# One buffer of 544 tokens per two heads, and the global queries' scores of a batch in one stage

## The chip, the cores and the metric

One NeuronCore of a Trainium2 chip. Five engines run queues of their own, in order: TensorE (PE in the profile, with its weight loads as PEld), VectorE (DVE), ScalarE (ACT), GpSimd (POOL) and SyncE (SP, which issues the DMAs). The metric is the time of one execution in microseconds (us), the median of three runs.

## The reference

Eight batches of eight heads, 512 local tokens (block `l`) and 32 global ones (block `g`), head size 64. A global query sees all 544 keys; a local query sees the 32 global keys and the local keys within 32 positions. The result, 544 tokens by 512 channels, goes through a gated layer with a convolution over tokens:

```python
s_g = scale * np.matmul(q_g, k_all.transpose(0, 1, 3, 2))
out_g = np.matmul(sm(s_g), v_all)
...
s_ll = np.where(mask, s_ll, -1000000000.0)
...
out_l = np.matmul(a_l, np.concatenate([v_g, v_l], axis=2))
...
h = np.maximum(x @ w_in, 0.0)
...
    conv_out += conv_w[k][None, None, :] * hp[:, k:k + S, :]
gate = 1.0 / (1.0 + np.exp(-conv_out))
return (h * gate @ w_out).astype(np.float32)
```

The weights arrive as 64-bit floats and are split on the chip into a high and a low part; the two products of the layer are sums of three products of such parts.

## The kernel before, in words

All work is cut into steps with short names. Per head `n`: local scores S (`SC`, for two heads at once: 32 matmuls of 128 columns, each on one of eight 64x32 parts of the array), mask and minimum M (`MA`, VectorE), exponential E (`EX`, ScalarE), transpose T (`TR`), its copy A. Per two heads: the sums NS, the value product P (`PV`, 32 matmuls of 64 columns on 128x32 parts), scaling N, transpose U, and then the layer's input: XH copies a rounded high part (ScalarE) and XL subtracts it for the low part (VectorE), both out of PSUM. Before, this is done twice, for the first 242 and the last 274 local columns (YH and YL are the second), into tiles `xh` and `xl` of 274 columns, `HW`; 13 of each exist.

The global queries go by groups of four heads: LG loads the queries, padded with zeros for the other head of a pair; G (`G`) makes their scores against four heads' keys with eight matmuls over all 128 rows, on four 128x32 parts, into two PSUM banks; GM scales them and takes the minimum (VectorE), GE the exponential, GN the reciprocal sums, GT six transposes, GC copies, GP 24 value matmuls, GO the scaling, GQ and GX put the result into the first 32 columns of the first half's input.

The layer runs by halves of 272 tokens, eight hidden units each: Z (`Z`, PZ in the tables) is twelve matmuls of 274 columns for unit `u`; RE the relu (ScalarE), C1, Ca and Cb the convolution (GpSimd, then VectorE twice), TH, and for two units GG the gate, GH and GL its two parts. The output is O, for each of four channel tiles in two halves Oa and Ob of twelve matmuls, then OE (copy) and ST (store). Units are numbered through: unit 0 to 15 are batch 0.

The weights come in eight chunks: WD (load), WA (ScalarE), WC (three VectorE instructions, L119 to L123), WH (ScalarE), WL (four VectorE instructions, L126 to L134). Units of a half need the `w_in` chunks two by two.

What sets the order: `plan` lists every step with what it waits for and which slots it takes (`SLOTS`), `arranged` plays them with costs and the tables POS, POS0 and WPOS, and `emit` writes them to the engines' queues in the order found. All psum tiles share eight banks. POS0, WPOS and `late` serve batch 0, POS the others.

Of the kernel before, what the change touches and what calls it, by code (L numbers as in the profile page):

```python
# [52 lines left out]
def attn_moe(ctx: ExitStack, tc: tile.TileContext, qk_d, vw_d, qg_d, w_in_d, w_out_d, cw_d, out_d):  # L53
# [28 lines left out]

    corner = const.tile([P, 2, 4, SG], F32, name="corner")
    nc.gpsimd.memset(corner, 0.0)
    for k, sign in enumerate((1, -1)):
        nc.gpsimd.affine_select(
            out=corner[:, k], in_=corner[:, k], pattern=[[sign * SG, 4], [sign, SG]], compare_op=ALU.is_ge, fill=NEG,
            base=0, channel_multiplier=-sign,  # L90
        )
# [57 lines left out]
    nc.sync.dma_start(out=cwr.rearrange("p n w -> p (n w)"), in_=cw_d)  # L149
    cw = drop(cwr)  # L150
    if wpe == 2:
        cw = const.tile([P, 3 * NFT], F32, name="cw")
# [1 line left out]
        w0, w1, t = cwr[:, :, 0], cwr[:, :, 1], cw.bitcast(U32)
        magnitude(w1, t)
        scaled_bits(w1, t, 0x7FFFF8)
        power(cwp, t)
        rest("v", f(cwp), w0, w1, cwp, 0)
        nc.vector.tensor_tensor(out=cw, in0=cw, in1=f(cwp), op=ALU.add)
# [761 lines left out]
```

## Time and profile before

| | |
|---|---|
| median of 3 runs | 595.16 us (594.88 to 595.27) |
| the profiled execution | 595.32 us, its span 593.5 us |
| busy: PE, PEld | 560.9 us (95%), 528.8 us (89%) |
| busy: DVE, ACT, POOL | 424.0 us (71%), 324.2 us (55%), 101.1 us (17%) |
| mean granted TensorE clock | 0.982 |

The span is the time from the first to the last instruction of the profiled execution; the execution's own time lies a little above it. Busy shares are averages over stages. A row of a timeline gives start, length, engine, line, operation, tiles, shapes and, in brackets, an idle time ahead of it and what ended it; rows of PE merge neighbours, a float32 matmul other than a transpose stands as two records (the eight of a G as x16), and a length ends where the last result is out, a little after the next stage starts. The difference of two starts is what a stage holds its engine.

### The profile page before, as it was taken

The numbers are of one execution on the slowest core, as the hardware profiler recorded it, in microseconds if no ns is written. First come the engines' busy times: TensorE is split into PE (matmuls) and PEld (weight loads), VectorE is DVE, ScalarE is ACT, GpSimd is POOL, SyncE is SP. The second block draws the span as 40 slices with busy tenths as digits, with TensorE's granted clock in tenths as the row PEclk, the third lists the DMA queues.
The fourth block names the chain that finished last, engine by engine and source line by source line (L and its number), as shares of the span: only waits on it lengthen the run. The fifth ranks groups of instructions, "written<-read, shape, count | busy, mean of one in ns | idle before, by whom it ended". The sixth has DMA issues, their size and how long they took to land.

```text
span 593.5 us, 20757 instructions
## 1 busy us (share of the span) xinstructions
PE 560.9 (95%) x8704; PEld 528.8 (89%) x8704; DVE 424.0 (71%) x1388; ACT 324.2 (55%) x994; POOL 101.1 (17%) x190
## 2 busy tenths in 40 slices
PE   5656997999999999999999999999999999999997
PEld 3345896999999999999999999999999999999997
DVE  4999999689477948577685858668584856565651
ACT  4954794676477666446565655555565543333320
POOL 6000242033012111121111012111101212221210
PEclk9977999899999999999999999999999999999999
DMA  6987334156234332123333222232412000000001
GB/s 254 390 286 313 95 118 170 39 204 223 91 135 153 107 134 98 56 110 108 135 108 145 100 78 94 100 144 97 146 63 75 20 22 20 29 20 29 30 29 47
DMA packets 22125, 68.46 MB, mean 115 GB/s; under 512 B 2576, under 2 KB 12816, under 8 KB 21008
## 3 DMA queue, kind: packets, MB, share of 16 engines
q1 hardware_dynamic: 22032, 67.14, 31.2%
q8 instruction: 68, 1.11, 0.8%
q14 instruction: 25, 0.20, 0.1%
HBM read 58.22 MB, written 8.91 MB: 113 GB/s over the span
## 4 chain that ended last, share of the span: by engine, by line
PE 84%; DVE 9%; ACT 2%; issue 1%; DMA 1%; POOL 0%; DVEq 0%
PE ps_o L523 32%; PE ps_h L460 31%; PE ps_v L325 5%; PE ps_s L264 4%; PE ps_t L304 4%; PE pv L341 2%; PE psg L278 2%; PE go L422 2%; PE gt L406 1%; DVE pr L285 1%; DVE t L484 1%; DMA vf<-vw 1%; DVE wt L123 1%; DVE raw L132 1%; ACT pr L295 1%
## 5 line engine op out<-in xcount | busy, mean ns | idle before, releaser
L460 PE MATMUL ps_h<-xh,w_in 128*128 128x274 f32 x1024 | 225.4, 298 | 2.8 <-DVE raw L132 1.3
L523 PE MATMUL ps_o<-g,w_out 128*128 128x272 f32 x1536 | 212.2, 290 | 0.0
L523 PEld LDWEIGHTS ps_o<-g,w_out 128*128 128x128 f32 x1536 | 200.0, 189 | 0.2
L460 PEld LDWEIGHTS ps_h<-xh,w_in 128*128 128x128 f32 x1024 | 171.9, 191 | 6.3 <-ACT g L212 1.4
L248 POOL TENSOR_SCALAR t<-hb,cw 128x272 f32<-128x272 f32 x128 | 79.9, 629 | 425.7 <-ACT hb L469 159.2
L460 PE MATMUL ps_h<-xl,w_in 128*128 128x274 f32 x512 | 149.5, 292 | 0.8 <-issue 0.8
L484 DVE SCALAR_TENSOR_TENSOR t<-hb,cw,t 128x272 f32<-128x272 f32 x256 | 125.7, 514 | 30.5 <-POOL t L248 29.1
L295 ACT ACTIVATE pr<-pr,negm 128x128 f32<-128x128 f32 x256 | 99.5, 391 | 47.7 <-DVE negm L285 47.7
L469 ACT ACTIVATE hb<-ps_h 128x273 f32<-128x273 f32 x128 | 50.8, 398 | 93.4 <-PE ps_h L460 91.9
L460 PEld LDWEIGHTS ps_h<-xl,w_in 128*128 128x128 f32 x512 | 98.1, 192 | 1.0 <-issue 1.0
L285 DVE CUSTOM_DVE_ANT_0 pr<-ps_s,mask 128x128 f32<-128x128 f32 x256 | 57.8, 285 | 25.6 <-PE ps_s L264 23.2
L212 DVE COPY o<-ps_o 128x272 f32<-128x272 f32 x64 | 28.0, 438 | 54.8 <-PE ps_o L523 54.6
L212 ACT CAST g<-t 128x544 fp32r<-128x544 f32 x64 | 40.9, 646 | 34.5 <-DVE t L498 22.6
L498 DVE SCALAR_TENSOR_TENSOR t<-t,hb 128x544 f32<-128x544 f32 x64 | 46.0, 719 | 14.3 <-ACT t L493 13.3
L493 ACT ACTIVATE t<-t 128x544 f32<-128x544 f32 x64 | 42.4, 663 | 15.0 <-DVE t L484 13.9
L212 ACT COPY a<-ps_t 128x512 f32<-128x512 f32 x64 | 37.0, 583 | 23.2 <-PE ps_t L304 23.0
L295 ACT ACTIVATION_READ_ACCUMULATOR pr<-pr,negm 128x1 f32 x256 | 48.3, 189 | 0.0
L264 PE MATMUL ps_s<-qk 64*32 64x128 f32 x2048 | 38.4, 283 | 8.4 <-DMA qk<-qk 5.8
L304 PE MATMUL ps_t<-ident,pr 128*128 128x128 f32 x256 | 43.0, 282 | 3.5 <-ACT pr L295 2.5
L215 DVE TENSOR_TENSOR g<-t,g 128x544 fp32r<-128x544 f32 x56 | 41.0, 737 | 6.8 <-ACT g L212 5.3
L264 PEld LDWEIGHTS ps_s<-qk 64*32 64x32 f32 x2048 | 29.9, 109 | 12.7 <-DMA qk<-qk 5.8
L304 PEld LDWEIGHTS ps_t<-ident,pr 128*128 128x128 f32 x256 | 31.1, 144 | 8.2 <-ACT pr L295 7.6
(70 smaller groups left out, 466.1 us busy)
## 6 DMA issues: line engine op xcount, KB each, us to landing
vf<-vw SPq DMA_DIRECT2D x32, 896.0 KB, 6.3
qk<-qk SPq DMA_DIRECT2D x32, 592.0 KB, 4.9
out<-o SPq DMA_DIRECT2D x64, 136.0 KB, 1.7
raw<-w_in SPq DMA_DIRECT2D x4, 1024.0 KB, 6.6
raw<-w_out SPq DMA_DIRECT2D x4, 1024.0 KB, 6.6
qgf<-qg SPq DMA_DIRECT2D x16, 64.0 KB, 2.0
cwr<-cw SPq DMA_DIRECT2D x1, 24.0 KB, 1.9
```

Source lines behind the costliest of these rows:

```text
L212: nc.scalar.copy(out=out, in_=in_) if choice(key) == "a" else eng(key).tensor_copy(out=out, in_=in_)
L248: nc.gpsimd.tensor_scalar(out=out, in0=in_, scalar1=by, scalar2=0.0, op0=ALU.mult, op1=ALU.add)
L264: nc.tensor.matmul(heads[n + j]["s"][b * SG : (b + 1) * SG, t, :], lhsT=qk[rows, i * SG : (i + 1) * SG], rhs=qk[rows, a : a + P], start=Tr ...
L285: nc.vector.tensor_tensor_reduce(out=pr[:, t, :], in0=st["s"][:, t, :], in1=mask[:, t].rearrange("p a c -> p (a c)"), op0=ALU.add, op1=ALU ...
L295: nc.scalar.activation(out=st["p"][:, t, :], in_=st["p"][:, t, :], func=AF.Exp, scale=-1.0, bias=st["m"][:, t : t + 1], accum_out=two["r"] ...
L304: nc.tensor.transpose(out=st["t"][:, t, :], in_=st["p"][:, t, :], identity=ident)
L460: nc.tensor.matmul(ps, lhsT=w[:, ft, ct, :], rhs=x, start=i == 0, stop=i == 3 * NCT - 1)
L469: nc.scalar.activation(out=o, in_=z, func=AF.Relu, scale=0.5)
L484: nc.vector.scalar_tensor_tensor(out=st["t"], in0=st["h"][:, k : k + HALF], scalar=cw[:, 3 * ft + k : 3 * ft + k + 1], in1=st["t"], op0=AL ...
L493: nc.scalar.activation(out=t, in_=t, func=AF.Tanh)
L498: nc.vector.scalar_tensor_tensor(out=t, in0=t, scalar=1.0, in1=h, op0=ALU.add, op1=ALU.mult)
L523: nc.tensor.matmul(ps, lhsT=w[:, mt, ft, :], rhs=g[:, ft, :], start=ft + i == 0, stop=ft == NFT - 1 and i == 2)
```

## The change

The input of the layer gets one pair of tiles per two heads, 544 columns wide (`x_of`); XH and XL handle 512 columns at once, YH and YL go away, and a unit reads a slice. Six such pairs exist in place of 13 half tiles. The half with the later tokens is now taken first (`TURN`). G serves a whole batch: the queries are no longer padded, each matmul contracts the 64 rows of one head, and sixteen matmuls on eight 64x32 parts fill four banks. The two groups that come out have heads mixed by pair and parity, so GP of a group needs the copies GC of both. GN scales the exponentials themselves, ahead of GT, in place of the weights that GO used. The mask is built half by VectorE, the convolution's taps (`taps`) are converted after the first weight chunk, and POS, POS0, WPOS, LATE and STAY have new values throughout, so that the written order differs from the first instruction on. `WAY` is all "v": a second way of splitting weights is in the code and not taken.

```diff
+        e = nc.vector if t < 2 else nc.gpsimd
...
+                e.tensor_copy(out=mask[rows, t, k], in_=corner[rows, int(local > i), b])
...
-                nc.gpsimd.tensor_copy(out=mask[rows, t, k], in_=corner[rows, int(local > i), b])
...
+    def taps():
...
-    def x_of(b, ct, half):
-        if (b, ct, half) not in xs:
-            xs[b, ct, half] = (xp.tile([P, HW], F32R, name="xh"), xp.tile([P, HW], F32R, name="xl"))
-        return xs[b, ct, half]
-
-    def outputs(n, half):
-
+    def x_of(b, ct):
+        if (b, ct) not in xs:
+            xs[b, ct] = (xp.tile([P, S], F32R, name="xh"), xp.tile([P, S], F32R, name="xl"))
+        return xs[b, ct]
+
+    def XH(n):
         b, h = divmod(n, H)
-        xh, xl = x_of(b, h // 2, half)
-        if half == 0:
-            return heads[n]["pv"][:, 0 : HW - SG], xh[:, SG:HW], xl[:, SG:HW]
-        return heads[n]["pv"][:, SL - HW : SL], xh, xl
-
-    def XH(n, half):
-        pv, xh, xl = outputs(n, half)
-        cp("XH", xh, pv)
-
-    def XL(n, half):
-        pv, xh, xl = outputs(n, half)
-        nc.vector.tensor_tensor(out=xl, in0=pv, in1=f(xh), op=ALU.subtract)
+        cp("XH", x_of(b, h // 2)[0][:, SG:S], heads[n]["pv"])
+
+    def XL(n):
+        b, h = divmod(n, H)
+        xh, xl = x_of(b, h // 2)
...
-        gr = groups[n // 4] = {}
-        gr["qgf"] = load.tile([P, 4, SG], F32, name="qgf", bufs=SLOTS["qg"])
-        nc.sync.dma_start(out=gr["qgf"], in_=qg_d[b, h // 4])
+        qg[n // H] = load.tile([P, 4, SG], F32, name="qgf", bufs=SLOTS["qg"])
+        nc.sync.dma_start(out=qg[n // H], in_=qg_d[n // H])
...
     def G(n):
 
-        gr = groups[n // 4]
-        gr["s0"] = bank([P, 480], "psg0")
-        gr["s1"] = bank([P, 64], "psg1")
-        for i, ps in enumerate((gr["s0"], gr["s1"])):
-            for j in range(4):
-                k = heads[n - 3 + j // 2 * 2]["qk"][:, SL:]
-                k = k[:, 608:672] if i else k[:, 0:640].rearrange("p (a c) -> p a c", c=P)[:, :, 0:96]
-                nc.tensor.matmul(ps[j * SG : (j + 1) * SG], lhsT=gr["qgf"][:, j, :], rhs=k, start=True, stop=True)
+
+        first = n - 7
+        g = [groups.setdefault(2 * (n // H) + j, {}) for j in range(2)]
+        for i, (name, w) in enumerate((("s0", 480), ("s1", 64))):
+            for j in range(2):
+                g[j][name] = bank([P, w], f"psg{i}")
+            for c in range(4):
+                k = heads[first + 2 * c]["qk"][:, SL:]
+                for j in range(2):
+                    rows = slice(j * D, (j + 1) * D)
+                    kj = k[rows, 608:672] if i else k[rows, 0:640].rearrange("p (a c) -> p a c", c=P)[:, :, 0:96]
+                    nc.tensor.matmul(
+                        g[j][name][c * SG : (c + 1) * SG], lhsT=qg[n // H][rows, c, :], rhs=kj, start=True, stop=True
+                    )
...
-        gr["w"] = small.tile([P, 2], F32, name="gw", bufs=SLOTS["pg"])
-        nc.vector.tensor_scalar(out=gr["w"], in0=whose, scalar1=sums, scalar2=None, op0=ALU.mult)
+        nc.vector.tensor_scalar(out=gr["pg"], in0=gr["pg"], scalar1=sums, scalar2=None, op0=ALU.mult)
...
         po = gr["po"] = bank([P, D], "go")
-        for c in range(6):
+        b, h = divmod(first, H)
+        for k in range(6):
             for j in range(4):
-                own = slice(j * SG, (j + 1) * SG)
-                v = heads[first + j // 2 * 2]["vf"][:, j % 2, VALUES.index(ONCE[c]), :]
-                nc.tensor.matmul(po[own], lhsT=gr["pgt"][:, c, own], rhs=v, start=c == 0, stop=c == 5)
+                c = h // 2 + j // 2
+                v = heads[first + j // 2 * 2]["vf"][:, j % 2, VALUES.index(ONCE[k]), :]
+                nc.tensor.matmul(
+                    po[j * SG : (j + 1) * SG], lhsT=groups[2 * b + j % 2]["pgt"][:, k, c * SG : (c + 1) * SG], rhs=v,
+                    start=k == 0, stop=k == 5,
+                )
 
     def GO(n):
 
         gr = groups[n // 4]
-        og = gr["og"] = att.tile([P, 2, D], F32, name="og", bufs=SLOTS["pg"])
-        po, w = gr["po"], gr["w"]
+        og = gr["og"] = att.tile([P, 2, D], F32, name="og", bufs=SLOTS["og"])
         nc.vector.tensor_tensor(
-            out=og, in0=po[:, None, :].to_broadcast([P, 2, D]), in1=w[:, :, None].to_broadcast([P, 2, D]), op=ALU.mult
+            out=og, in0=gr["po"][:, None, :].to_broadcast([P, 2, D]), in1=whose[:, :, None].to_broadcast([P, 2, D]),
+            op=ALU.mult,
...
+    def half_of(hh):
+        return (hh + TURN) % 2
...
-            xh, xl = x_of(b, ct, half)
+            xh, xl = (x[:, half * (S - HW) : half * (S - HW) + HW] for x in x_of(b, ct))
...
-    ps=8, x=13, hb=2, qk=3, vf=3, qg=2, p=4, r=3, a=4, n=2, pg=1, pgt=1, t=2, o=2, wt=1, g0=2, g1=2,
+    ps=8, x=6, hb=2, qk=5, vf=3, qg=2, p=4, r=3, a=4, n=2, pg=2, pgt=2, og=2, t=2, o=2, wt=1, g0=2, g1=2,
...
-    LQ=-3.56, LG=-53.13, LV=12.71, S=-3.9, M=7.61, E=46.84, NS=-11.03, T=-16.54, A=-39.33, P=-1.74, N=0.2, U=-7.02,
...
+    LQ=-13.92, LG=-68.69, LV=2.61, S=-2.17, M=37.43, E=93.64, NS=-82.9, T=-1.82, A=-40.59, P=-24.11, N=-52.26,
...
+TURN = 1
+
+WAY = "vvvvvvvv"
...
-            for half, x in enumerate("XY"):
-                name = f"x{b},{h // 2},{half}"
-                at_n(x + "H", [("U", e)] + [("YH", e - 2)] * (e > 0), [("x", name)], [f"pv{p}"], i=e)
-                at_n(x + "L", [(x + "H", e)], [], [f"pv{p}", name], i=e)
-        if n % 4 == 3:
-            ks = [f"qk{p - 1}", f"qk{p}"]
-            at_n("G", [("LQ", n - 3), ("LQ", n - 1), ("LG", n - 3)], [("ps", f"ga{g}"), ("ps", f"gb{g}")], ks + [f"qg{g}"])
-            at_n("GM", [("G", n)], [("pg", f"pg{g}")], [f"ga{g}", f"gb{g}"])
-            at_n("GE", [("GM", n)], [], [f"pg{g}"])
-            at_n("GN", [("GE", n)], [], [f"pg{g}"])
-            at_n("GT", [("GE", n)], [("ps", f"gt{g}"), ("ps", f"gu{g}")], [f"pg{g}"])
-            at_n("GC", [("GT", n)], [("pgt", f"pgt{g}")], [f"gt{g}", f"gu{g}"])
-            at_n("GP", [("GC", n), ("LV", n - 3), ("LV", n - 1)], [("ps", f"go{g}")], [f"pgt{g}", f"vf{p - 1}", f"vf{p}"])
-            at_n("GO", [("GP", n), ("GN", n)], [], [f"go{g}", f"pg{g}"])
-            at_n("GQ", [("GO", n)], [("ps", f"gq{g}")], [f"pg{g}"])
-            at_n("GX", [("GQ", n), ("XL", n - 3), ("XL", n - 1)], [], [f"gq{g}", f"x{b},{h // 2 - 1},0", f"x{b},{h // 2},0"])
+            at_n("XH", [("U", e)] + [("XH", e - 2)] * (e > 0), [("x", f"x{b},{h // 2}")], [f"pv{p}"], i=e)
+            at_n("XL", [("XH", e)], [], [f"pv{p}", f"x{b},{h // 2}"], i=e)
+        if n % H == H - 1:
+            ks = [f"qk{p - 3 + c}" for c in range(4)]
+            banks = [("ps", f"g{x}{g - 1 + j}") for x in "ab" for j in range(2)]
+            at_n("G", [("LQ", n - 7 + 2 * c) for c in range(4)] + [("LG", n - 7)], banks, ks + [f"qg{b}"])
+            for i in (n - 4, n):
+                k = i // 4
+                at_n("GM", [("G", n)], [("pg", f"pg{k}")], [f"ga{k}", f"gb{k}"], i=i)
+                at_n("GE", [("GM", i)], [], [f"pg{k}"], i=i)
+                at_n("GN", [("GE", i)], [], [f"pg{k}"], i=i)
+                at_n("GT", [("GN", i)], [("ps", f"gt{k}"), ("ps", f"gu{k}")], [f"pg{k}"], i=i)
+                at_n("GC", [("GT", i)], [("pgt", f"pgt{k}")], [f"gt{k}", f"gu{k}"], i=i)
+            for i in (n - 4, n):
+                k, q = i // 4, i // 2
+                vs = [f"vf{q - 1}", f"vf{q}"]
+                at_n("GP", [("GC", n - 4), ("GC", n), ("LV", i - 3), ("LV", i - 1)], [("ps", f"go{k}")], [f"pgt{g - 1}", f"pgt{g}"] + vs, i=i)
+                at_n("GO", [("GP", i)], [("og", f"og{k}")], [f"go{k}"], i=i)
+                at_n("GQ", [("GO", i)], [("ps", f"gq{k}")], [f"og{k}"], i=i)
+                at_n("GX", [("GQ", i), ("XL", i - 3), ("XL", i - 1)], [], [f"gq{k}", f"x{b},{i % H // 2 - 1}", f"x{b},{i % H // 2}"], i=i)
...
-    qg = np.zeros((B, 2, 2, D, 4, SG), np.float32)
-    for j in range(4):
-        qg[:, :, j % 2, :, j] = q_g[:, j::4].transpose(0, 1, 3, 2)
-    qg = qg.reshape(B, 2, P, 4, SG)
+    qg = c(q_g.reshape(B, 4, 2, SG, D).transpose(0, 2, 4, 1, 3)).reshape(B, P, 4, SG)
```

PE in the steady part, just around a G; `psg` are its banks, `ps_v` those of P, `ps_s` of S, `ps_h` of Z. Before:

```order
L264 MATMUL ps_s<-qk 32x128 x32
L325 MATMUL ps_v<-vf,a 32x64 x32
L278 MATMUL psg_3526<-qk,qgf 32x480 x4
L278 MATMUL psg_3527<-qk,qgf 32x64 x4
L460 MATMUL ps_h<-xh,w_in_151 128x274
```

And in the changed kernel, where one such place comes per batch:

```order
L352 MATMUL ps_v<-vf,a 32x64 x32
L303 MATMUL psg_4456<-qk,qgf 32x480
L303 MATMUL psg_4457<-qk,qgf 32x480
...
L303 MATMUL psg_4466<-qk,qgf 32x64
L303 MATMUL psg_4467<-qk,qgf 32x64
...
L486 MATMUL ps_h<-xh,w_in_141 128x274
...
L285 MATMUL ps_s<-qk 32x128 x64
```

Eight matmuls into two banks, twice a batch, have become sixteen into four banks, alternating between the banks of the two groups; S moved from ahead of P to behind the next Z, and two of it stand together.

PE ahead of the first Z, where the units start (`go` is GP, `gq` is GQ, `pv` is U, `gt` is GT). Before:

```order
L341 MATMUL pv<-ident,n 128x128 x8
L406 MATMUL gt<-ident,pg 96x128 x4
...
L422 MATMUL go<-vf,pgt_161 32x64 x24
L264 MATMUL ps_s<-qk 32x128 x64
L436 MATMUL gq<-place,og 128x64
L460 MATMUL ps_h<-xh,w_in_151 128x274
```

And in the changed kernel:

```order
L442 MATMUL go<-vf,pgt_152 32x64
L331 MATMUL ps_t<-ident,pr 128x128 x8
L459 MATMUL gq<-place,og 128x64
L331 MATMUL ps_t<-ident,pr 128x128 x4
L352 MATMUL ps_v<-vf,a 32x64 x96
L368 MATMUL pv<-ident,n 128x128 x8
L331 MATMUL ps_t<-ident,pr 128x128 x8
L486 MATMUL ps_h<-xh,w_in_141 128x274
```

The first Z now stands behind three P and five T of which most belong to batch 1.

SP, the first loads. Before:

```order
L149 DMA cwr<-cw 128x48
L242 DMA qgf<-qg 128x128 x2
L229 DMA qk<-qk 128x1184 x2
L174 DMA raw<-w_in 128x2048
L229 DMA qk<-qk 128x1184
```

And in the changed kernel:

```order
L263 DMA qgf<-qg 128x128
L252 DMA qk<-qk 128x1184 x2
L174 DMA raw<-w_in 128x2048
L252 DMA qk<-qk 128x1184 x2
L174 DMA raw<-w_out 128x2048
```

The taps and one load of queries no longer stand ahead of the first keys, and all four pairs of batch 0 are asked for before the second weight chunk.

## Rows read from the trace of the kernel before

**Rows 1.** Two stretches: length, busy PE, PEld, DVE, ACT, POOL, PEclk, DMA.

```profile
15.00:105.00 90.00, 69.27 (x1450) 57.63 (x1446) 87.29 (x259) 61.97 (x192) 13.91 (x15) 0.91 0.61 227
105.00:590.00 485.00, 483.43 (x7044) 465.59 (x7043) 330.05 (x1079) 256.22 (x783) 77.72 (x121) 1.00 0.26 91
```

**Rows 2.** Timeline of PE in the steady part: start, length, instructions.

```profile
334.18 1.10 PE L278 MATMUL psg<-qk,qgf 128*32 128x480 f32 x16
335.21 0.40 PE L460 MATMUL ps_h<-xh,w_in 128*128 128x274 f32 x1
...
336.85 0.60 PE L304 MATMUL ps_t<-ident,pr 128*128 128x128 f32 x4
337.29 0.60 PE L341 MATMUL pv<-ident,n 128*128 128x128 f32 x4
...
358.44 1.66 PE L523 MATMUL ps_o<-g,w_out 128*128 128x272 f32 x12
359.94 0.29 PE L460 MATMUL ps_h<-xh,w_in 128*128 128x274 f32 x1
...
361.46 1.66 PE L523 MATMUL ps_o<-g,w_out 128*128 128x272 f32 x12
...
366.07 1.16 PE L264 MATMUL ps_s<-qk 64*32 64x128 f32 x64
367.16 1.10 PE L325 MATMUL ps_v<-vf,a 128*32 128x64 f32 x64
368.08 1.10 PE L278 MATMUL psg<-qk,qgf 128*32 128x480 f32 x16
```

**Rows 3.** Timeline of all engines at the start.

```profile
2.11 0.91 SPq L229 DMA_DIRECT2D qk<-qk  x2
...
7.97 0.29 DVE L285 CUSTOM_DVE_ANT_0 pr<-ps_s,mask 128x128 f32<-128x128 f32 x1 [3.37 <-PE ps_s L264]
```

**Rows 4.** Timeline of DVE in the first 24 us.

```profile
14.00 0.65 DVE L373 TENSOR_SCALAR_CACHE_REDUCE pg<-psg 128x480 f32<-128x480 f32 x1
...
14.91 0.16 DVE L315 TENSOR_SCALAR sums<-sums 128x8 f32<-128x8 f32 x1
...
15.23 0.64 DVE L119 TENSOR_SCALAR wt<-wt 128x1024 f32<-128x1024 f32 x1
...
16.64 1.22 DVE L123 SCALAR_TENSOR_TENSOR wt<-raw,wt 128x1024 uint32<-128x1024 uint32 x1
17.78 0.28 DVE L285 CUSTOM_DVE_ANT_0 pr<-ps_s,mask 128x128 f32<-128x128 f32 x1
...
19.47 0.69 DVE L126 TENSOR_SCALAR wt<-wt 128x1024 uint32<-128x1024 uint32 x1
...
23.21 0.28 DVE L285 CUSTOM_DVE_ANT_0 pr<-ps_s,mask 128x128 f32<-128x128 f32 x1
```

**Rows 5.** Groups of instructions by line and shape, the whole run.

```profile
L484 DVE SCALAR_TENSOR_TENSOR t<-hb,cw,t 128x272 f32<-128x272 f32 x256 | 125.7, 514 | 30.5 <-POOL t L248 29.1
...
L498 DVE SCALAR_TENSOR_TENSOR t<-t,hb 128x544 f32<-128x544 f32 x64 | 46.0, 719 | 14.3 <-ACT t L493 13.3
...
L333 DVE TENSOR_TENSOR n<-ps_v,sums 128x512 f32<-128x512 f32 x32 | 21.8, 683 | 2.0 <-PE ps_v L325 1.8
```

**Rows 6.** Timeline of PE: first hidden unit, and unit 12.

```profile
53.57 0.37 PE L460 MATMUL ps_h<-xh,w_in 128*128 128x274 f32 x1
...
110.89 0.29 PE L460 MATMUL ps_h<-xh,w_in 128*128 128x274 f32 x1
```

**Rows 7.** Timeline of DVE in the steady part.

```profile
336.07 0.65 DVE L373 TENSOR_SCALAR_CACHE_REDUCE pg<-psg 128x480 f32<-128x480 f32 x1
```

**Rows 8.** Timeline of all engines at the end.

```profile
568.99 0.29 PE L460 MATMUL ps_h<-xh,w_in 128*128 128x274 f32 x1
...
574.11 0.73 DVE L215 TENSOR_TENSOR g<-t,g 128x544 fp32r<-128x544 f32 x1 [0.71 <-ACT g L212]
```

**Rows 9.** One stretch of 5 us, columns as in rows 1.

```profile
55.00:60.00 5.00, 4.02 (x24) 2.35 (x24) 4.86 (x17) 2.88 (x10) 1.05 (x1) 0.50 0.27 107
```

More of the change, by code (lines that the diff above doesn't have):

```diff
@@ L70, in attn_moe @@
     make_identity(nc, ident)
+    corner = const.tile([P, 2, 4, SG], F32, name="corner")
+    nc.gpsimd.memset(corner, 0.0)
+    for k, sign in enumerate((1, -1)):
+        nc.gpsimd.affine_select(
+            out=corner[:, k], in_=corner[:, k], pattern=[[sign * SG, 4], [sign, SG]], compare_op=ALU.is_ge, fill=NEG,
+            base=0, channel_multiplier=-sign,
+        )
+    mask = const.tile([P, 4, 4, SG], F32, name="mask")
+    nc.vector.memset(mask, 0.0)
+    for i in range(NB):
+        t, b = divmod(i, 4)
+        e = nc.vector if t < 2 else nc.gpsimd
+        rows = slice(b * SG, (b + 1) * SG)
+        for k in range(4):
+            block = FIRST[i] + k
+            local = block - block // 4
+            if block % 4 == 3 or local == i:
+                continue
+            if abs(local - i) > 1:
+                e.memset(mask[rows, t, k], NEG)
+            else:
+                e.tensor_copy(out=mask[rows, t, k], in_=corner[rows, int(local > i), b])
     place = const.tile([P, 2, SG], F32, name="place")
@@ L153, in attn_moe @@
         cwp = const.tile([P, 3 * NFT], U32, name="cwp")
[L154 to L159, printed above, removed]
+    def taps():
+        if wpe == 2:
+            w0, w1, t = cwr[:, :, 0], cwr[:, :, 1], cw.bitcast(U32)
+            magnitude(w1, t)
+            scaled_bits(w1, t, 0x7FFFF8)
+            power(cwp, t)
+            rest(f(cwp), w0, w1, cwp, 0)
+            nc.vector.tensor_tensor(out=cw, in0=cw, in1=f(cwp), op=ALU.add)
     def eng(key):
@@ L219, in attn_moe @@
     groups = {}
+    qg = {}
     xs = {}
@@ L463, in RE @@
     def RE(u):
-        half = u // NFT % 2
+        half = half_of(u // NFT)
         o = hid[u]["h"][:, 1 - half : HW - half]
@@ L495, in GG @@
     def GG(u):
-        t, half = hid[u]["two"], u // NFT % 2
+        t, half = hid[u]["two"], half_of(u // NFT)
         h = hb[u // 2 % SLOTS["hb"]][:, :, half + 1 : half + 1 + HALF]
@@ L725, in plan, with weight @@
     return ops
+def weight(i):
+    return ("WL" if WAY[i] == "v" else "WT", i)
 def units(op, late, b):
@@ L730, in units @@
         hh = 2 * b + half
-        x = [f"x{b},{ct},{half}" for ct in range(NCT)]
+        half = (half + TURN) % 2
+        x = [f"x{b},{ct}" for ct in range(NCT)]
         for ft in range(NFT):
@@ L736, in at_u @@
                 op(key, u, late(H + u // 2 + u % 2 * 0.5, b) + (POS if b else POS0)[key], b > 0, *more)
[L738 to L739 removed]
+            ready = [("XL", 8 * b + h) for h in range(0, H, 2)]
+            ready += [("GX", 8 * b + 3), ("GX", 8 * b + 7)] * (half == 0) + [weight(ft // 2)]
             at_u("PZ", ready + [("PZ", u - 1)] * (u > 0), [("ps", f"h{u}"), ("h", f"h{u}h")], x)
```

124 lines of the change are left out of this document (60 added, 64 removed).

## The prediction

> **What bounds the kernel now.** I read the stretches first [rows 1]. From 15 to 105 us VectorE is busy 87.3 of 90 us and TensorE only 69.3; from 105 to 590 us TensorE is busy 483.4 of 485 us and VectorE 330. So there are two kernels to think about: a start paced by VectorE, which splits the eight weight chunks while it serves the first two batches, and a long rest paced by TensorE alone. Then I read TensorE's timeline in the steady part [rows 2] for what each kind of stage holds the engine, from one start to the next: a global score stage G 1.03 us (334.18 to 335.21), a transpose T 0.44, an output half O 1.50, a hidden unit Z 1.52, a local score stage S 1.09, a value stage P 0.92. In that part every microsecond taken from TensorE's queue comes off the end, as long as no wait replaces it.
>
> **G, which the change halves.** Before, a G served four heads with eight matmuls on four array parts: per part one of 480 and one of 64 columns, 544 columns in 1.03 us, 1.9 ns a column. After, one G of sixteen serves eight heads on eight parts, again 544 columns per part. Whether eight parts run side by side is shown by S, which already uses these 64x32 parts: 32 matmuls of 128 columns are 512 columns per part, in 1.09 us with a change of array shape behind them [rows 2]; if only four ran at once it would be 1024 columns, 1.9 us at G's rate. At S's 2.13 ns a column the new G takes 1.16 us, at the old rate 1.03; I take 1.10, which leaves room for the change of shape that now stands between P and G (both had 128x32 parts before). The other end is 2.06, no gain. Per batch 2.06 - 1.10 = 0.96 us. [...]
>
> **Whole buffers.** XH, XL for 242 and 274 columns become one for 512. An instruction of VectorE starts 0.08 us before the record of the one ahead ends (16.64 + 1.22 against 17.78 is such a case), so I take mean less 0.08. The nearest row to the new XL is the 128x512 one from PSUM, 683 ns [rows 5]: 0.60. This saves VectorE little, and ScalarE and VectorE wait for TensorE in the rest, so there I cost it at nothing. The buffer now lives until both halves of a batch are multiplied, and six exist. In the written order two O (3.0 us) stand between the last Z of a batch and the first of the next, while two buffers are refilled: a relu, two ScalarE copies, then XL, about 0.4 + 0.5 + 0.5 + 0.6 = 2.0 us with the pitches above. Covered, by 1 us; without that cover, up to 2 us a batch.
>
> **Other edits at nothing.** Normalizing the exponentials (128x544, in SBUF) replaces a small one: between 0 and +0.6 us (the 128x512 row) on VectorE, 16 times, in a queue that is 68% busy from 105 us; in the start it is in the sum below at 0.7 for the whole step. GT now waits for it, but in the steady order some 8 us of S, O and Z stand between. Query loads are 8 instead of 16, early and small. Taking the second half first lets Z start without the global tokens; its price is in the walk below. At the end four O (6.0 us) stand behind the last Z before its gates are needed, instead of ten; the chain from that Z's end (568.99 + 0.29) to the last gate (574.11 + 0.73) was 5.6 us [rows 8], so it fits, by 0.4.
>
> **The start, walked along VectorE.** It is saturated, so its sum gives the time. The first qk load is issued two small loads earlier, 0.9 us by the pair of issues at 2.11, so the first mask step M comes at 7.97 - 0.9 = 7.1 [rows 3]. The mask copies, now split between VectorE and GpSimd, mostly run before that. Ahead of the first Z, VectorE's written order has: five weight chunks, each 2.55 + 3.74 = 6.29 (15.23 to 17.78, 19.47 to 23.21 [rows 4]), 31.5; M of 16 heads, 0.845 each (17.78 to 19.47 holds two), 13.5; six sums NS at 0.32, 1.9; five N at 0.60, 3.0; four XL at 0.60, 2.4; two GM at 0.91 (14.00 to 14.91), 1.8; two GN at 0.7, 1.4; the taps (1.6), GO and GX (1.0) 2.6. Sum 58.1; with 1.5 us for two waits I see (last mask tiles; the taps' ScalarE step) Z can start at 7.1 + 58.1 + 1.5 = 67. Before it started at 53.57 [rows 6], with M of 8 heads done, not 16.
>
> Between that and unit 12 (the thirteenth Z) VectorE's order has two weight chunks, 12.6; 16 convolution steps at 0.43, 6.9, and four gates GG at 0.64, 2.6 (means less 0.08 [rows 5]); four M 3.4; two N, two XL 2.4; two GM 1.8; two GN 1.4; NS and GX 1.6; together 32.7. That opens the hidden buffers for units 10 and 11, and so the bank of unit 12, at 99.7 + about 0.5. TensorE's own work from Z0 to unit 12 is 12 Z 18.2, 6 T 2.6, 2 S 2.2, 2 O 3.0, G 1.1, P 0.9, 2 U 0.9, and GT, GP, GQ about 2.2: 31.1, so 98.1 without waits; but ahead of the first Z its queue waits for VectorE's GO of the second group (at about 56 us in the walk) and then for the last XL, so it idles much of 44 to 67 and will begin slow. [...] So 100.6; with both limits this close I take **101 for the start of unit 12**. Before it was 110.89.
>
> **The sum.** By then, counted in the two orders, the changed kernel has done four O, one P and one U fewer, four T and one GT more: 6.0 + 0.9 + 0.4 - 1.8 - 0.6 = 4.9 us still owed. From there six batches save 0.96 in G, 5.8 us. For VectorE coming late to the scores I add 0.1 a batch, 0.6. The profiled execution took 595.3 us (span 593.5 and 1.8 around it; the median of the runs is 0.1 lower): 595.3 - 9.9 + 4.9 - 5.8 + 0.6 = **585.1 us**.
>
> **Rivals.**
> *The start gives its part back.* For it: the walk assumes VectorE never waits, though ScalarE was busy too and the fourth V load is only issued once the first GP frees a buffer. Against it: from 15 to 105 us VectorE idled 2.7 us in all. If it loses 3 to 6 us more, the gain is mostly G's: 588 to 591. It would have to lose 10 to lose all: then 595 and above.
> *G's row halves do not overlap.* No gain in G, 585.1 + 5.8 = 590.9. S speaks against it.
> *Banks (slower).* G now fills four of the eight PSUM banks at once, and the S stage for two pairs, four banks more, follows after a single Z. The banks come free only as VectorE reads them in two GM of 0.91 each. Before, GM began at 336.07, 0.86 us after G ended at 335.21 [rows 7]. If VectorE begins L after G's end, the second half of S needs its banks at 1.52 + 1.0 = 2.5 us and gets them at L + 1.8: a wait of L - 0.7, behind which all of TensorE stands. At L = 0.86 that is 0.2 a batch. The gain is gone at 10.2 / 6 = 1.7 a batch, L = 2.4; at L = 3 the time is 585.1 + 6 x 2.3 = 599. VectorE's idle third speaks against so late a start, but its queue is in order and gates and output copies stand ahead. [...]
> *Late start (slower).* Z begins 13 us later than before. If the order's other engines delay unit 12 past 111, say to 115, the time is 599.
>
> **Chances.** Forecast (579 to 588) 0.60; start gives back 0.17; halves do not overlap 0.04; banks 0.09; late start 0.07; better than 579, if less clock is lost, 0.03. Range 578 to 592, which takes in the first three. A change within 0.2% (1.2 us) is what a measurement here cannot tell from none: 0.04. Faster: 0.60 + 0.17 + 0.04 + 0.03 and a little of the banks, 0.85; slower 0.11.
>
> **What would show it.** G's sixteen matmuls in about 1.1 us, eight of them in the steady part; first Z near 67 and unit 12 near 101 us; no TensorE wait on VectorE behind G; a low granted clock just before 67 us. Wrong if: G takes 2 us, S behind G waits in each batch, VectorE shows more than 5 us idle between 15 and 100 us, or the last O wait for a gate.

## The result and the profile after

The changed kernel took 589.73 us (median of 4, 589.26 to 591.01) beside 595.02 us for the kernel before on the same chip: ratio 0.9905, 95% interval 0.9886 to 0.9924. The forecast was 585.1 us, so it is faster as forecast, but by 5.3 us where 10.2 were expected. The profiled execution has a span of 587.2 us (593.5 before).

First the two stretches, columns as in [rows 1]:

```profile
15.00:105.00 90.00, 71.07 (x1339) 59.28 (x1338) 85.77 (x277) 66.39 (x210) 11.71 (x12) 0.89 0.56 212
105.00:587.00 482.00, 479.01 (x7101) 464.72 (x7099) 323.40 (x1037) 247.79 (x722) 66.82 (x125) 1.00 0.26 91
```

The picture is that of before: VectorE (third figure) full in the start, TensorE (first) full in the rest. From 105 us on no wait of TensorE is listed any more; the few microseconds missing in its 479.01 of 482 lie at the end, behind the last matmul.

TensorE's timeline where the units start and at unit 12, beside [rows 6]:

```profile
66.76 0.38 PE L486 MATMUL ps_h<-xh,w_in 128*128 128x274 f32 x1
...
104.02 0.43 PE L459 MATMUL gq<-place,og 128*128 128x64 f32 x2 [0.63 <-DVE og L451]
104.52 0.39 PE L486 MATMUL ps_h<-xh,w_in 128*128 128x274 f32 x1
```

The first Z stands where it was forecast (66.76 for 67). Unit 12 stands at 104.52, forecast 101, before 110.89. What TensorE waits for just ahead of it is VectorE's GO (`og`), which stands in VectorE's queue right behind the gate that the prediction named. In a second profiled execution of the changed kernel (after2, below) unit 12 stood at 104.97. From unit 12 to the end of the span both kernels take the same: 593.5 - 110.89 = 482.6 and 587.2 - 104.52 = 482.7.

One batch in the steady part, TensorE and then VectorE, beside [rows 2] and [rows 7]:

```profile
330.73 1.15 PE L303 MATMUL psg<-qk,qgf 64*32 64x480 f32 x32
331.81 0.39 PE L486 MATMUL ps_h<-xh,w_in 128*128 128x274 f32 x1
...
333.52 2.06 PE L285 MATMUL ps_s<-qk 64*32 64x128 f32 x128
```

```profile
331.88 0.65 DVE L393 TENSOR_SCALAR_CACHE_REDUCE pg<-psg 128x480 f32<-128x480 f32 x1
```

G holds TensorE 1.08 us (330.73 to 331.81) where two G held it 2.06. GM begins 0.07 us behind G, and the two S, which need G's banks, start without a wait. G comes every 67.22 us (263.51, 330.73, 397.95).

The end, beside [rows 8]: last Z and last gate.

```profile
568.59 0.29 PE L486 MATMUL ps_h<-xh,w_in 128*128 128x274 f32 x1
...
573.73 0.72 DVE L237 TENSOR_TENSOR g<-t,g 128x544 fp32r<-128x544 f32 x1 [0.71 <-ACT g L234]
```

The gate is there 574.45 - 568.88 = 5.6 us after that Z, and TensorE's matmuls run on without a gap: the four O cover it, as forecast.

VectorE in the start: its list of waits up to 67 us (us in total, times, longest), and three rows of its timeline behind that.

```profile
DVE cw L120 <- ACT cw L113: 1.2, 1, 1.2
DVE wt L120 <- ACT wt L113: 0.9, 2, 0.5
DVE pr L312 <- PE ps_s L285: 0.8, 1, 0.8
DVE pr L312 <- POOL mask L95: 0.7, 1, 0.7
```

```profile
82.11 1.14 DVE L397 TENSOR_TENSOR gnegm<-gnegm 128x1 f32<-128x1 f32 x1
...
99.33 1.23 DVE L133 SCALAR_TENSOR_TENSOR raw<-raw 128x1024 f32<-128x1024 uint32 x1
100.59 2.27 DVE L134 SCALAR_TENSOR_TENSOR w_out<-raw,wt 128x1024 fp32r<-128x1024 f32 x1
```

The wait of 0.8 lies ahead of the first M, at 7.05. An instruction on 128x1 takes 1.14 us here (its twin at 81.19 takes 0.16), and a step of a weight chunk 2.27 (1.23 for the same step of other chunks). These are counted as busy. The experiments ask why.

### The profile page after: what moved, and what is told of

It reads as the page before. It is cut to its first block, busy times and chain, and to the rows that moved or that the text cites. A ratio compares the mean times of both kernels' runs of the same rounds, so it can differ in the third digit from the quotient of the medians.

```text
span 587.2 us, 20661 instructions
## 1 busy us (share of the span) xinstructions
PE 558.8 (95%) x8704; PEld 530.8 (90%) x8704; DVE 419.9 (72%) x1373; ACT 322.9 (55%) x962; POOL 85.6 (15%) x175
## 4 chain that ended last, share of the span: by engine, by line
PE 82%; DVE 13%; ACT 3%; POOL 1%; issue 1%; POOLq 0%; ACTq 0%
PE ps_o L549 33%; PE ps_h L486 31%; PE ps_v L352 5%; PE ps_s L285 4%; PE ps_t L331 3%; PE pv L368 2%; DVE pr L312 2%; PE go L442 2%; DVE wt L124 1%; PE gt L425 1%; DVE raw L133 1%; ACT pr L322 1%; PE psg L303 1%; DVE w_in L134 1%; DVE wt L121 1%; DVE wt L120 1%
## 5 line engine op out<-in xcount | busy, mean ns | idle before, releaser
L510 DVE SCALAR_TENSOR_TENSOR t<-hb,cw,t 128x272 f32<-128x272 f32 x256 | 123.2, 497 | 54.8 <-POOL t L269 53.1
L269 POOL TENSOR_SCALAR t<-hb,cw 128x272 f32<-128x272 f32 x128 | 67.1, 527 | 443.1 <-ACT hb L495 323.3
L312 DVE CUSTOM_DVE_ANT_0 pr<-ps_s,mask 128x128 f32<-128x128 f32 x256 | 56.6, 284 | 5.0 <-PE ps_s L285 4.4
L331 PE MATMUL ps_t<-ident,pr 128*128 128x128 f32 x256 | 45.9, 297 | 2.4 <-ACT pr L322 1.4
L285 PE MATMUL ps_s<-qk 64*32 64x128 f32 x2048 | 36.1, 282 | 6.1 <-DMA qk<-qk 6.1
L331 PEld LDWEIGHTS ps_t<-ident,pr 128*128 128x128 f32 x256 | 33.2, 151 | 8.6 <-ACT pr L322 7.8
L352 PE MATMUL ps_v<-vf,a 128*32 128x64 f32 x2048 | 36.6, 226 | 0.7 <-DVE pg L393 0.6
```

The source lines that it names most:

```text
L269: nc.gpsimd.tensor_scalar(out=out, in0=in_, scalar1=by, scalar2=0.0, op0=ALU.mult, op1=ALU.add)
L285: nc.tensor.matmul(heads[n + j]["s"][b * SG : (b + 1) * SG, t, :], lhsT=qk[rows, i * SG : (i + 1) * SG], rhs=qk[rows, a : a + P], start=Tr ...
L312: nc.vector.tensor_tensor_reduce(out=pr[:, t, :], in0=st["s"][:, t, :], in1=mask[:, t].rearrange("p a c -> p (a c)"), op0=ALU.add, op1=ALU ...
L331: nc.tensor.transpose(out=st["t"][:, t, :], in_=st["p"][:, t, :], identity=ident)
L352: nc.tensor.matmul(ps[rows, t, j, :], lhsT=heads[n + j]["a"][:, t, rows], rhs=heads[n]["vf"][:, j, VALUES.index(FIRST[4 * t + b]), :], sta ...
L510: nc.vector.scalar_tensor_tensor(out=st["t"], in0=st["h"][:, k : k + HALF], scalar=cw[:, 3 * ft + k : 3 * ft + k + 1], in1=st["t"], op0=AL ...
```

## The experiments

The theory at this point: in the rest the gain is G's, on TensorE's path; the start gains less than forecast, because VectorE, which paces it, is held up by GpSimd. Rivals: G's time is hidden, and the start alone gains; or the start is set by something other than VectorE; and, for the other sign, the banks. Times are medians; kernels of one group ran on one chip beside the kernel before.

**First group (before: 595.23 us).**

*g4: G on four parts again.*

```diff
-                    rows = slice(j * D, (j + 1) * D)
-                    kj = k[rows, 608:672] if i else k[rows, 0:640].rearrange("p (a c) -> p a c", c=P)[:, :, 0:96]
+                    kj = k[:, 608:672] if i else k[:, 0:640].rearrange("p (a c) -> p a c", c=P)[:, :, 0:96]
...
-                        g[j][name][c * SG : (c + 1) * SG], lhsT=qg[n // H][rows, c, :], rhs=kj, start=True, stop=True
+                        g[j][name][c * SG : (c + 1) * SG], lhsT=qg[n // H][:, j, c, :], rhs=kj, start=True, stop=True
```

> The changed kernel with G alone as it was: sixteen matmuls on four 128x32 array parts, the queries padded with zeros to 128 rows, in the same place in the same order. If TensorE's queue paces the rest, each of the six G behind unit 12 takes about 2.06 us instead of 1.08 and the end moves by 6 x 0.98 = 5.9 us, to about 595.6; the two G in the start cost nothing, because VectorE paces the start (up to 1.96 more if it does not). If the gain came from the new start alone and G's time is hidden behind other work, the time stays at 589.7.

The padded queries are loaded as before, twice the bytes. Measured 594.49 us, ratio 0.9993 (0.9975 to 1.0011). TensorE at G:

```profile
264.96 2.07 PE L302 MATMUL psg<-qk,qgf 128*32 128x480 f32 x32
266.96 0.40 PE L485 MATMUL ps_h<-xh,w_in 128*128 128x274 f32 x1
```

G holds TensorE 2.00 us, and a batch takes 68.03 to 68.08 us instead of 67.22 (but for one of 71.60, in which TensorE stopped for 1.8 us and had a granted clock of 0.56 and 0.58 behind it, from 308 to 312 us; such stops are treated below): 0.83 a batch, 5.0 in six. Unit 12 stands at 104.06, where G of the first two batches doesn't matter. So undoing this one part takes back 4.8 to 5.1 of the 5.3 us (594.49 less the changed kernel's 589.73 and after2's 589.38). G's time is on the path, and nearly all of the gain is G's.

*vec_gm and vec_xl: the same VectorE work in two places.* In vec_gm the 480-column instruction of the first GM is issued four more times; in vec_xl each XL is written twice.

```diff
+        for i, (ps, sl) in [(0, (gr["s0"], slice(0, 480)))] * (4 if n >= 16 and n % 8 == 3 else 0) + list(
```

```diff
+        for _ in range(2 if b >= 2 else 1):
+            nc.vector.tensor_tensor(out=xl[:, SG:S], in0=heads[n]["pv"], in1=f(xh)[:, SG:S], op=ALU.subtract)
```

> The changed kernel with four more VectorE reads of the 480-column scores ahead of the first GM of each batch from the third on (same results, written again), 4 x 0.58 = 2.3 us. In the trace GM begins 0.07 us after G ends, so L becomes about 2.4. The rival called banks says: S behind G waits L - 0.7 = 1.7 us in each of six batches, 10 us in all, so about 600. If VectorE's slack takes it and the banks are no limit even then: 589.7. A wait of some length on TensorE behind G, on VectorE, would show the rival's mechanism even where its price is off.

> Control to the one before: the same amount of VectorE work, 4 x 0.60 = 2.4 us a batch from the third on, but in another place (each XL is written twice with the same values). TensorE alone paces the rest: 589.7, at most 0.6 more. If any lateness of VectorE reaches TensorE: as much as with the additions ahead of GM.

Measured 603.14 us for vec_gm (ratio 1.0135, 1.0099 to 1.0170) and 589.52 for vec_xl (0.9899, 0.9867 to 0.9931). A line of TensorE's list of waits in vec_gm, and where VectorE's own first GM, behind the four added reads, begins in the batch whose G ends at 269.20:

```profile
PE ps_s L285 <- DVE pg L395: 7.8, 5, 1.6
```

```profile
272.08 0.66 DVE L395 TENSOR_SCALAR_CACHE_REDUCE pg<-psg 128x480 f32<-128x480 f32 x1
```

One read more costs 0.70 us, not 0.58, so L was 2.88, and S waited 1.57 in each of five batches listed; a quiet batch took 69.2 us, 2.0 more. Of the rest of the 13 us, 2.4 lie in a wait of GT for the normalizing and 1.2 in a stop without a releaser (the profile names nothing that ended it); some 0.4 a batch beside the wait was not taken apart. The banks are a real mechanism, as the rival had it, and VectorE's lateness matters there and hardly at XL, the other place tried: 2.4 us a batch there cost 0.13 a batch (67.35 instead of 67.22). The changed kernel escapes because GM starts at once.

*vec_start: 2.16 us more on VectorE at 24 us.*

```diff
+            for _ in range(3 if i == 4 else 0):
+                nc.vector.tensor_scalar(
+                    out=f(wf[i]), in0=f(wf[i]), scalar1=LEAST, scalar2=MOST, op0=ALU.max, op1=ALU.min
+                )
```

> The changed kernel with three more clamps of 0.72 us (same values again) on VectorE in the second weight chunk, at about 24 us: 2.16 us. If VectorE's queue sets the start from 7 us to unit 12, unit 12 moves from 104.5 to 106.7 and the end by as much, to 591.9. If TensorE's queue or the loads set it, with slack on VectorE, the end moves by less than 0.5: 589.7 to 590.2.

Measured 591.24 us (0.9940, 0.9915 to 0.9966). Unit 12:

```profile
106.55 0.40 PE L490 MATMUL ps_h<-xh,w_in 128*128 128x274 f32 x1
```

The changed kernel has 104.52 and 104.97, so it comes 1.6 to 2.0 later, and the span (589.3) 1.7 to 2.1 longer. VectorE's queue sets the start from 24 us on, nearly one for one.

**Second group (before: 595.55 us).**

*after2: the changed kernel again.*

> The changed kernel once more, as the yardstick for the three beside it: 589.7. If the long VectorE instructions between 66 and 104 us (the second least-value step of GM at 82.1, 1.14 us where its twin takes 0.16; the last step of the seventh and last weight chunks at 100.6, 2.27 where its twins take 1.23) are what the program makes of it and no chance, they stand here again within 0.05 us.

Measured 589.38 us (0.9907, 0.9876 to 0.9939). The long instructions, with GpSimd's beside them:

```profile
82.33 1.36 POOL L237 TENSOR_TENSOR g<-t,g 128x544 fp32r<-128x544 f32 x1 [3.17 <-ACT g L234]
...
100.22 2.01 POOL L237 TENSOR_TENSOR g<-t,g 128x544 fp32r<-128x544 f32 x1 [6.46 <-ACT g L234]
```

```profile
82.54 1.17 DVE L397 TENSOR_TENSOR gnegm<-gnegm 128x1 f32<-128x1 f32 x1
...
101.04 2.27 DVE L134 SCALAR_TENSOR_TENSOR w_out<-raw,wt 128x1024 fp32r<-128x1024 f32 x1
```

They recur within 0.03 us. GpSimd's GL runs from 82.33 to 83.69, and VectorE's tiny instruction that began in it ends at 83.71; GL ends at 102.23, and 1.08 us later the chunk's step, which alone takes 1.23. That looks like waiting for GpSimd's end. In the second pair GpSimd is late as well (2.01 for 1.36): it began inside the step ahead, of 1.23 us from 99.77. Not every GL does this: the one between them runs from 90.89 to 92.25 in the changed kernel, beside M steps (`pr<-ps_s,mask`), and these keep their 0.28 us. Why the two should hold each other up these rows don't show; whether GL is the cause, the next two runs ask.

*gl_zero and gl_vec: no GL on GpSimd at these two places.*

```diff
+        if u in (1, 5):
+            nc.gpsimd.memset(f(gl)[:, ft - 1 : ft + 1, :], 0.0)
+            return
```

and in gl_vec

```diff
+        if u in (1, 5):
+            nc.vector.tensor_tensor(
+                out=gl[:, ft - 1 : ft + 1, :], in0=hid[u]["two"], in1=f(gh)[:, ft - 1 : ft + 1, :], op=ALU.subtract
+            )
+            return
```

> The changed kernel with the two GL (low part of the gates) of units 1 and 5, which GpSimd computes in the start, replaced by GpSimd memsets to zero: the low part of four hidden blocks of one half batch is left out. Theory: a two-input GpSimd instruction holds up a two-input VectorE instruction that meets it; without it the two long VectorE instructions fall to 0.16 and 1.23, unit 12 starts 2.0 us earlier (102.5 instead of 104.5) and the end is 2.0 earlier, 587.7. Rival: these instructions are long for a reason on VectorE itself (a late operand, its queue): they stay long and the time stays at 589.7.

> The changed kernel with the GL of units 1 and 5 on VectorE instead of GpSimd. By the theory of held-up instructions VectorE saves 2.0 us and pays 2 x 0.65: unit 12 0.7 earlier, time 589.0. If GpSimd has nothing to do with the long instructions, VectorE only pays: unit 12 1.3 later, 591.0.

Measured 588.06 us for gl_zero (0.9885, 0.9844 to 0.9926) and 588.38 for gl_vec (0.9887, 0.9849 to 0.9926). The same two instructions and unit 12 in gl_zero:

```profile
82.55 0.30 DVE L397 TENSOR_TENSOR gnegm<-gnegm 128x1 f32<-128x1 f32 x1
...
100.17 1.23 DVE L134 SCALAR_TENSOR_TENSOR w_out<-raw,wt 128x1024 fp32r<-128x1024 f32 x1
```

```profile
103.07 0.39 PE L486 MATMUL ps_h<-xh,w_in 128*128 128x274 f32 x1
```

The instructions shrink, unit 12 comes 1.9 us earlier than in after2 and the span is 1.8 shorter (585.8 for 587.6). In gl_vec unit 12 stands at 104.03, 0.94 earlier, and the span is 0.9 shorter. Beside the first execution of the changed kernel (104.52) unit 12 comes 1.5 and 0.5 earlier. The intervals of the ratios overlap with after2's, so the times alone would not settle it; the lengths of the two instructions, which agree within 0.03 us from execution to execution, do. Holding up by these two GL is shown as the cause of 1.9 us of VectorE's time (0.87 and 1.04), of which 1.5 to 1.9 show at unit 12.

*clamp_pool: one of VectorE's steps on idle GpSimd.*

```diff
             magnitude(raw[i][:, :, 1], wf[i])
+            nc.gpsimd.tensor_scalar(
+                out=f(wf[i]), in0=f(wf[i]), scalar1=LEAST, scalar2=MOST, op0=ALU.max, op1=ALU.min
+            )
...
-            scaled_bits(raw[i][:, :, 1], wf[i], 0x7FF000 if WAY[i] == "v" else 0x7FFFF8)
+            scaled_bits(raw[i][:, :, 1], wf[i], 0x7FF000 if WAY[i] == "v" else 0x7FFFF8, False)
```

> The changed kernel with the clamp of each weight chunk (one-input, 128x1024, 0.72 us on VectorE) moved to GpSimd, which stands idle from 9 to 71 us, right behind ScalarE's magnitude. If VectorE's work sets the start, seven clamps before unit 12 give back up to 5.0 us; GpSimd's own clamp takes perhaps twice as long and now stands between ScalarE and VectorE, and one-input GpSimd work stretched VectorE instructions by 0.17 in the trace, so I expect 3 us: unit 12 near 101.5, time 586.7. Rival: the longer chain and held-up VectorE instructions eat it: 589.7 or above.

Measured 605.90 us (1.0183, 1.0129 to 1.0236), a miss. GpSimd, then VectorE behind it:

```profile
26.63 3.62 POOL L191 TENSOR_SCALAR wt<-wt 128x1024 f32<-128x1024 f32 x1 [10.73 <-ACT wt L113]
30.28 0.70 DVE L122 TENSOR_SCALAR wt<-wt 128x1024 uint32<-128x1024 uint32 x1 [2.61 <-POOL wt L191]
```

GpSimd's clamp takes 3.62 us, five times VectorE's 0.69, where the expectation took perhaps twice without a row for it, and VectorE waits for it 17 us in all (4.3 at most in one chunk); unit 12 moves to 119.26.

**Third group (before: 595.65 us).**

*taps_late and norm_act: towards a better version.* taps_late is gl_vec with the taps' VectorE steps moved (their ScalarE step stays where it was); norm_act adds the second edit, for batches 0 and 1.

```diff
+    def WC(i):
+        if i == 6:
             taps()
```

```diff
+            nc.scalar.activation(out=gr["pg"], in_=gr["pg"], func=AF.Copy, scale=sums)
```

> The changed kernel with the GL of units 1 and 5 on VectorE, as before, and VectorE's eight small steps on the convolution taps moved from behind the third weight chunk (45.0 us) to the fifth (59 us), so that VectorE no longer waits 1.2 us there for ScalarE's step. If VectorE's queue sets the start, unit 12 comes 1.2 us earlier than with the two GL alone (102.8 instead of 104.0) and the time is 587.2. If something else is late next (the query pieces S, ScalarE), less than 0.4 comes: 588.0 to 588.4.

> The one before, and in the first two batches the normalizing of the exponentials (128x544, 0.42 us on VectorE, four times before unit 12) done by ScalarE. VectorE's queue then holds 1.7 us less: unit 12 near 101.3, time 585.6. Against it: ScalarE, in order and busy 66 of 90 us in the start, now waits for VectorE's reciprocal and does 0.65 more each time; if that delays the exponentials of S for VectorE, nothing is gained: 587.2 or more.

Measured 587.10 us for taps_late (0.9859, 0.9839 to 0.9879) and 587.49 for norm_act (0.9861, 0.9842 to 0.9879). Unit 12 of taps_late:

```profile
102.03 0.37 PE L487 MATMUL ps_h<-xh,w_in 128*128 128x274 f32 x1
```

That is 2.0 us earlier than in gl_vec. The wait for the taps, 1.2 us in gl_vec, is gone from VectorE's list; the other 0.8 was not taken apart. It is the fastest version found, 8.5 us below the kernel before. norm_act gains nothing: unit 12 is at 102.91, and VectorE's waits for ScalarE (1.2 us in two, 0.8 in a third; in taps_late 0.3) take the place of its work.

*gm2: two more reads instead of four.*

```diff
-            * (4 if n >= 16 and n % 8 == 3 else 0)
+            * (2 if n >= 16 and n % 8 == 3 else 0)
```

> The changed kernel with two instead of four more VectorE reads of the 480-column scores ahead of the first GM of each batch from the third on: 1.16 us, so L is 1.2. With four, S waited 1.57 us, where L - 0.7 gave 1.7. If the wait is L less a constant, it is 0.4 to 0.5 now, in each batch, and the time some 3 us above the changed kernel's, 592.5. If the banks bind only beyond a larger L, S waits nothing: 589.5.

Measured 599.54 us (1.0063, 1.0042 to 1.0083), more than expected; its profile says why. S waits 0.17 us in each batch (L was 1.48), and a quiet batch takes 67.82 us, 0.6 more than the changed kernel, 3.6 in six. The other 6 us come from two stops of TensorE, for which the profile names no releaser, in two of the batches (69.70 and 72.32 us). The longer one, and stretches around it:

```profile
343.66 2.91 PE L551 MATMUL ps_o<-g,w_out 128*128 128x272 f32 x12 [2.73 <-issue]
```

```profile
335.00:340.00 5.00, 4.83 (x173) 3.86 (x172) 4.74 (x19) 1.46 (x4) 0.30 (x2) 1.00 0.48 168
340.00:343.60 3.60, 0.93 (x27) 0.49 (x8) 3.42 (x15) 3.18 (x12) 0.26 (x1) 1.00 0.99 380
343.60:346.00 2.40, 2.34 (x11) 2.34 (x12) 0.00 (x0) 0.00 (x0) 0.00 (x0) 0.56 0.31 128
346.00:348.00 2.00, 2.00 (x13) 2.00 (x13) 1.39 (x10) 1.35 (x5) 0.00 (x0) 0.67 0.06 18
```

TensorE stands for 2.73 us while the transfers run at 380 GB/s, and then works at a granted clock of 0.56 and 0.67 up to 348 us: 4.5 us lost in that batch (72.32 less 67.82). On the banks, S waits 0.17 at L = 1.48 and 1.57 at L = 2.88: a wait of L - 1.31. For gm2 0.4 to 0.5 were expected.

*before2: the kernel before again.*

> The kernel before once more, to see whether TensorE's stop of 2.6 us in the middle of a score stage at 100.9 us, for which the trace names no releaser, belongs to the program. If it does, it stands in the same stage again, and unit 12 starts at 110.9 within 0.5 us. If it is chance, it is gone or elsewhere, and unit 12 starts near 108.

One time, 595.37 us. The stop in the kernel before, and below it in this second execution:

```profile
100.25 0.63 PE L264 MATMUL ps_s<-qk 64*32 64x128 f32 x23
103.48 0.88 PE L264 MATMUL ps_s<-qk 64*32 64x128 f32 x41 [2.60 <-issue]
```

```profile
100.12 0.63 PE L264 MATMUL ps_s<-qk 64*32 64x128 f32 x23
103.94 1.06 PE L264 MATMUL ps_s<-qk 64*32 64x128 f32 x41 [3.19 <-issue]
```

It stands behind the same 23 matmuls: it belongs to the program. Unit 12 starts at 111.34, 0.45 us later behind a stop that is 0.59 longer. This execution had another stop, of 3.8 us, that ended at 40.3 us, where TensorE in the first one waited for VectorE until 43.6.

## Why the forecast was right in sign and half in size

**G.** Right. 1.08 us for 1.10 forecast, eight parts side by side; the rival that the row halves don't overlap is out. What a change of array shape costs by itself, for which the forecast left room, no run shows. On the path it gave 0.83 a batch, where 0.96 less 0.10 for lateness was forecast: 5.0 us for 5.2. That no stage had to wait for VectorE (the 0.10) but some 0.1 a batch went elsewhere among the stages makes the two errors nearly cancel.

**The start.** This is the step that failed, by 3.5 us at unit 12, and it was a term of the walk that was mis-sized, not its mechanism: vec_start shows that VectorE's queue does pace it. M began at 7.05 (forecast 7.1). The last XL for the first unit ended at 68.3 instead of 67, because VectorE waited 2.8 us on the way (0.7 for masks, 0.9 and 1.2 for ScalarE) and I had set 1.5. From the end of that XL to the gate that opens the hidden buffers of units 10 and 11, VectorE took 35.2 us instead of 32.7: the two instructions held up by GL (0.98 and 1.04) and three that took 1.40 instead of 1.23 beside GpSimd's C1 (0.5). These three look held in the same way, though C1 has one input, where gl_zero's theory names two, and no run took a C1 away: each ends 1.07 us after a C1 does (C1 at 72.15, 77.30 and 78.73), as the step beside GL ends 1.08 after it in after2; they met C1 only near its end. That the first Z began at 66.76 in spite of the late XL is luck: its first matmuls read pairs that were there, and the one that reads the last `xl` began at 68.60. I had taken durations from rows where GpSimd was idle, although the trace of before has such a case in the same part, GpSimd's row above VectorE's:

```profile
87.08 1.80 POOL L215 TENSOR_TENSOR g<-t,g 128x544 fp32r<-128x544 f32 x1 [6.94 <-ACT g L212]
87.70 2.26 DVE L123 SCALAR_TENSOR_TENSOR wt<-raw,wt 128x1024 uint32<-128x1024 uint32 x1
```

So the rival "the start gives its part back" described the outcome (588 to 591, the gain mostly G's), with 3.8 us lost on VectorE; of the causes I named for it, ScalarE's load has a part in the first 1.3 us, and the fourth V load none. My sign for it, more than 5 us of idle VectorE, would have missed it: idle time from 15 to 105 us was 4.2 us, because a held instruction counts as busy.

**What the start did gain.** 5.9 to 6.8 us at unit 12, by which two executions are compared. Just ahead of its unit 12 the kernel before had its stop of 2.60 us and a low clock behind it:

```profile
100.00:102.00 2.00, 0.88 (x47) 0.53 (x36) 2.00 (x6) 0.77 (x3) 0.00 (x0) 1.00 1.02 420
...
104.00:106.00 2.00, 2.00 (x32) 1.80 (x18) 0.35 (x4) 0.00 (x0) 0.00 (x0) 0.77 0.24 75
106.00:108.00 2.00, 2.00 (x11) 2.00 (x10) 0.17 (x1) 1.19 (x2) 0.49 (x1) 0.50 0.01 3
108.00:110.00 2.00, 2.00 (x16) 2.00 (x16) 1.59 (x10) 0.69 (x3) 0.00 (x0) 0.88 0.00 0
```

At a clock (last figure but two) of 0.77, 0.50 and 0.88, TensorE loses 0.46 + 1.00 + 0.24 = 1.7 us of those six, with the stop 4.3.

The changed kernel has such a stop too (2.49 us, at 48 us), but there TensorE has to wait for VectorE's GO afterwards anyway, until 57.5:

```profile
50.51 1.44 PE L442 MATMUL go<-vf,pgt 128*32 128x64 f32 x42 [2.49 <-issue]
...
57.48 0.69 PE L459 MATMUL gq<-place,og 128*128 128x64 f32 x2 [3.62 <-DVE og L451]
```

That the start's gain is mostly this is read from the rows; no run here took the stop out of the kernel before.

**The sum.** The low clock near the first Z was there (0.50 from 68 to 70 us), behind it rather than ahead. No run of the changed kernel shows the 2.5 us that the forecast sets between 98.1 and 100.6 for a slow clock: 0.88, 0.50 and 0.77 from 66 to 72 us make 1.7 us there; 2.5 is what the 0.50 of [rows 9] makes over its five microseconds. The work still owed at unit 12 I counted as 4.9 us. From equal rests (482.6 and 482.7), with 5.0 us saved by G and 1.6 us in two further stops of 0.8 that only the kernel before has in its rest, it comes out as 6.7. The matmuls counted behind unit 12 confirm the owed stages, and at the lengths of the kernel before they are 5.2 us. The rest is stages that take longer or shorter beside new neighbours: summed from start to start behind unit 12, G holds TensorE 5.9 us less in all, and the other stages together 2.3 more (Z 2.0, O 1.6 and P 1.3 longer, S 1.9 and T 1.6 shorter among them); 5.2 + 2.3 - 5.9 - 1.6 = 0.0, as the equal rests ask. Why each stage changed is not shown. So start and debt cancel (-6.4 and +6.7, forecast -9.9 and +4.9), and between the two profiled executions G's 5.0 and the two stops' 1.6 are the gain. The 1.6 are luck: no term of the sum had them.

**The other rivals.** Late start: out, 104.5 is well before 115. Banks: no wait in the changed kernel, L = 0.07; the mechanism exists, with a wait of L - 1.31 where I had L - 0.7, since S needs the bank of the first GM and not of both (in vec_gm its wait ends at 272.89, and the second GM begins at 273.00). GM itself kept its time under the new layout, 0.92 us (331.88 to 332.80) beside 0.91 before [rows 4]. Since a batch lost another 0.43 us beside the wait in both kernels, the measured gain in G, 0.83 a batch, would be gone at L = 1.7 by this line. Whole buffers and tail: covered, as forecast; from 105 us on TensorE shows no wait. Whether taking the later half first costs or saves anything by itself was not tried: in the same order of instructions the other half would be read before its global columns are written.

## What to carry to other kernels

Where one engine's queue paces a stretch, walk that queue, but take durations from rows that have the same neighbour running: two VectorE instructions that met a GL of GpSimd took 1 us longer here (1.14 for 0.16, 2.27 for 1.23), more than doing that GL on VectorE costs (0.64 from start to start in gl_vec). Before crediting a change of order with a gain, look for stops in the old order that the new one merely moves to a harmless place, and for work that the new order still owes at the point of comparison. Taking four PSUM banks at once cost nothing here, because the reader of the first bank began 0.07 us behind; measure that distance, and how much it may grow. When an engine stops without a releaser, count its instructions up to the stop, in several runs (below).
